# Layer two's last 256 rows in two chunks of 128, with one kept copy of the first MLP weight

## The chip, the cores and the metric

The kernel runs on one core of one Trainium2 chip. The metric is the device time of one execution in microseconds (us); the lower, the better.

## The reference

A transformer block is applied twice to x (2048 rows of 512 numbers), with the same weights both times:

```
x = x + A(layernorm(x))        A: 32 heads of width 16, softmax attention over all 2048 rows, then wo
x = x + B(layernorm(x))        B: relu(x @ w1) @ w2, inner width 1792
x = x + A(layernorm(x))
x = x + B(layernorm(x))
return x
```

Inputs and outputs are bfloat16. The attention needs 2 x 32 x 2048 x 2048 exponentials, which makes it the larger part of the work.

## The kernel before

**Tiles and chunks.** Rows are held in 16 tiles of 128 (`x_t`). A *chunk* is a run of row tiles that goes through attention, output projection, layer norm and MLP together. `chunks[l, j]` gives the first tile and the number of tiles. Layer one has four chunks of 512 rows. Layer two has two of 512 and then four of 256, (1,2) to (1,5); `LAST = 5` names the last one.

**Attention.** The attention of a chunk is cut into 8 *segments* (`t`) of four heads each, one head in each quarter of the array's rows; a segment runs over all 16 blocks of 128 keys. A *unit* is one head with 512 columns of scores: one key block for a chunk of 512 rows, two key blocks for a chunk of 256 (`both = QS // sg["w"]`). Three units fill a *slot*: TensorE computes the scores with 32-row weights (L1396), and ScalarE takes the exponential of up to 1536 columns in one instruction (L1405, `e`). In about half of the slots one of the three units goes to VectorE instead: it makes the exponential out of integer steps, two units at a time as a *pair* (`lin` L1090, `step` L1131, `cube` L1142 and L1146), and ScalarE's instruction is then 1024 wide. Such a unit is called a *half* below, as in the code. TensorE then multiplies by the values with 32-column weights (L983) and sums into the single PSUM bank `ps_o`; a pair needs three such products for one.

**End of a segment.** `finish_segment` copies `ps_o` to `u` (L897), sends the sums to a compact tile `c` by a DMA on SyncE's queue (L902), takes the reciprocal (L924), sends it back (L925) and spreads it over the partitions into `r`. The spreading is a DMA on GpSimd's queue (L927) or, for a segment that is `quick`, a shuffle on VectorE (L937). A multiplication (L913) then writes `ot`. There are three buffers `u`, `r` and `c`.

**The filler.** Output projection, layer norm and MLP of a chunk are cut into groups, which are put into the gaps that TensorE has while the attention of the next chunk runs (L446). `h_group` makes the first MLP product for one, or two, blocks of 128 inner columns; its weight `w1` comes from HBM, block by block, into four buffers (`load_w1`, L714), for every chunk again. `z_group` makes the second product with the resident `w2` (L768 adds it to x).

**The order.** All engines' instructions are put in order while the program is built, by a planner with a clock of its own for TensorE, VectorE and ScalarE. It holds constants for what a DMA takes: `C_LAG` for `c`, `U_LAG` for a quick `r`, `R_LAG` for an `r` that is spread by DMA. A VectorE step is put where its inputs are due by these constants. A planner's wrong guess leaves a wait in the order of an engine. It also decides for each pair whether VectorE can finish it before its segment ends. If TensorE is planned to be too idle, scores are computed more than once in a slot.

**The end.** The last chunk's projection, layer norm and MLP have no attention beside them. They are written out by hand (L1440 to L1528): the projection and the last segment's normalization (`direct`, L944 to L949), the statistics and the root, `half_part` (the second product of the second row tile of the chunk before, which TensorE does meanwhile), transposes, and then the MLP, one block of 128 inner columns after the other: `h` for block `ft`, relu on VectorE or ScalarE in turn, and the second product for block `ft - 1`. The `w1` blocks 4 to 13 for this are kept in the buffers of layer one's keys (`kt01`, `kt2`), which are free by then. They are loaded during the MLP of chunk (1,3), one block after each `h_group` (L747, `w1_to_load`).

Of the kernel before, what the change touches and what calls it, by code (L numbers as in the profile page):

```python
# [12 lines left out]
BF16 = mybir.dt.bfloat16  # L13
# [12 lines left out]
def kernel(  # L26
# [11 lines left out]
    P = 128  # L38
# [3 lines left out]
    S, D = x_flat.shape  # L42
# [4 lines left out]
    NF = DFF // P  # L47
    NTT = S // P
    NKB = S // P
    NDC = D // P  # L50
    QS = 512
# [25 lines left out]
    PE_TO_DVE, DVE_TO_PE, ACT_TO_PE, PE_TO_ACT = 220.0, 180.0, 240.0, 222.0  # L77
    DVE_TO_DVE, EVAC = 112.0, 612.0
    FLOOR = 0.56
    C_LAG, R_LAG, U_LAG = 3600.0, 10500.0, 3000.0  # L80
    VLAG = 1
    X_ISSUE, X_LAG = 1400.0, 7500.0
    RSTD_LAG = 4000.0
# [214 lines left out]
    def put_evac(cost, fn):  # L298
        evac.append((cost, now_pe[0] + PE_TO_DVE, fn))
# [159 lines left out]

    chunks = {(l, j): (j * TPC, TPC) for l in range(2) for j in range(NQS)}  # L460
    HALF = TPC // 2
    for n in range(4):
        chunks[1, 2 + n] = (2 * TPC + n * HALF, HALF)
    LAST = 5

    def columns(l, j):

# [118 lines left out]
    def ln_groups(tag, dst, at_column, n, war):  # L586
        groups = []
        for i in range(0, n, 2):
            hold = {}

            def piece(k):
                if not k % 2:
                    hold["b"] = bank()
                half = hold["b"].bitcast(BF16)[:, k % 2 * D : (k % 2 + 1) * D]
                ln_transpose(tag, k, half)
                if not k % 2:
                    return
                pt = hold["b"].bitcast(BF16).rearrange("p (i c f) -> p c i f", i=2, c=NDC)

                def fin():  # L600
                    a = at_column + (k - 1) * P
                    nc.vector.tensor_copy(
                        out=dst[:, :, a : a + 2 * P].rearrange("p c (i f) -> p c i f", i=2), in_=pt
                    )
                    for of in (k - 1, k):
                        mark(("xnT", tag, of))

                put_evac(609, fin)

            groups.append(  # L610
                group(
                    [(1.3, lambda k=k, piece=piece: piece(k)) for k in (i, i + 1)],
                    [("xT", tag, k) for k in (i, i + 1)] + [("xnT", tag, k) for k in (i, i + 1)],
                    [("xn", tag, k) for k in (i, i + 1)] + war,
                )
            )
        return groups

    def each(n, *key):
        return [key + (i,) for i in range(n)]  # L620
# [88 lines left out]

    def load_w1(n):  # L710

        if n < len(chunks) * NF - NF + NW1:
            ft = n % NF
            nc.sync.dma_start(  # L714
                out=w1buf[n % NW1][:],
                in_=B_w1[:, ft * P : (ft + 1) * P].rearrange("(c p) f -> p c f", p=P),
            )
            mark(("w1", n), "pe", 4000.0)

    w1_to_load = deque()  # L720

    def h_group(l, j, ft, war):
        n = (l * NQS + j) * NF + ft
        xj, a, w = columns(l, j)

        number = QS // w
        fts = range(ft, ft + number)
        made_here = [("h", l, j, f) for f in fts]

        def fin(b):  # L730
            out = htp[ft // 2][:, ft % 2 : ft % 2 + number, a : a + w]
            sums = b.rearrange("p (f q) -> p f q", f=number)
            if ending[0]:
                nc.scalar.activation(out=out, in_=sums, func=ACTF.Relu)
            else:
                nc.vector.tensor_scalar(  # L736
                    out=out, in0=sums, scalar1=0.0, scalar2=None, op0=ALU.max
                )
            for key in made_here:
                mark(key)  # L740

        def after():
            for f in range(number):
                load_w1(n + f + NW1)
            if w1_to_load:
                home, of = w1_to_load.popleft()
                nc.sync.dma_start(  # L747
                    out=home,
                    in_=B_w1[:, of * P : (of + 1) * P].rearrange("(c p) f -> p c f", p=P),
                )  # L750

        return mm_group(
            [
                (w1buf[(n + f) % NW1][:, c, :], xnT[xj][:, c, a : a + w])
                for f in range(number) for c in range(NDC)
            ],
            fin, made_here,
            each(w // P, "xnT", ("ln2", l, j)) + war + [("w1", n + f) for f in range(number)],
            after=after, wide_by=w, sums=number,
        )  # L760

    def z_group(l, j, i):
# [18 lines left out]
    def before(l, j):  # L781

        if (l, j) == (0, 0):
            return None
        if not j:
            return 0, NQS - 1
        rows = chunks[l, j][0] % TPC
        return max(
            (l, b) for b in range(j)
            if chunks[l, b][1] == TPC or chunks[l, b][0] % TPC == rows  # L790
        )

    w1_last = []
# [1 line left out]
    def rest_of_chunk(l, j):  # L795

        if (l, j) == (1, LAST - 2):
            for ft in range(NF):
                home = (
                    w1buf[((l * NQS + LAST) * NF + ft) % NW1] if ft < NW1  # L800
                    else (kt01 + kt2)[(ft - NW1) // 2][:, ft % 2, :].rearrange(
                        "p (c f) -> p c f", c=NDC
                    )
                )
                w1_last.append(home)
                if ft >= NW1:
                    w1_to_load.append((home, ft))
        b = before(l, j)
        xj, a, w = columns(l, j)
        n = w // P  # L810
        war_h = each(chunks[b][1], "z", *b) if b else []
        work[0:0] = [o_group(l, j, i) for i in range(n)] + ln_groups(
            ("ln2", l, j), xnT[xj], a, n, []
        )
        gs = [h_group(l, j, ft, war_h) for ft in range(0, NF, QS // w)]
        gs += [z_group(l, j, i) for i in range((l, j) == (1, LAST - 1), n)]
        if l == 0:
            if not by_dma(("ln1", 1, j)):
                gs += ln_groups(("ln1", 1, j), xnT[j], 0, TPC, [])
            gs.append(k_group(1, 0, j))  # L820
            gs += [v_group(1, kb) for kb in range(j * TPC, (j + 1) * TPC)]
            gs += [k_group(1, T, j) for T in range(1, 4)]
        return gs
# [43 lines left out]
    def finish_segment(sg, last):  # L867
# [50 lines left out]
                mark(("ot", l, j, t, i))  # L918

        ended[l, j] = ended.get((l, j), 0) + 1  # L920
        quick = ended[l, j] == NT or sg["load"] is not None and sg["busy"]

        def recip():
            nc.vector.reciprocal(out=c, in_=c)  # L924
# [35 lines left out]
        if last:  # L960
            last_steps.append(direct)
        elif sg is segs[-2]:
            task(3100, direct_all, ots + [("m", n)], war + [("u", n)])
        else:
            task(165, recip, [("r", n)], [("c", n)], place=0)
            ready = ("r", n)
            if quick:
                task(200 + 1.05 * width, spread, [("spread", n)], [ready])
                ready = ("spread", n)
            task(105 + 1.1 * width, lambda: mul(0, width), ots + [("m", n)], [ready] + war)  # L970
# [588 lines left out]
```

The softmax here doesn't subtract the row's maximum and nothing guards it: scores larger than these inputs give would overflow.

## Time and profile before

| what | value |
|---|---|
| time, median of 4 runs | 1586.87 us (1586.18 to 1589.21) |
| time of the profiled execution, and its span | 1586.18 us, 1584.3 us |
| ScalarE busy | 1545.3 us, 98% of the span |
| VectorE busy | 1506.3 us, 95% |
| TensorE busy | 1428.1 us, 90% |
| exponentials on ScalarE (L1405) | 1366: 663 of 1536 columns, 702 of 1024, one of 512 |
| from the end of the last exponential to the end of the span | 27.2 us |

The profile is a page on one execution. Its first part gives each engine's busy time, a later one the *chain of waits* that ended last, followed back from the last instruction. The *groups* list instructions by code line and shape with their busy time in us, the mean length of one in ns, and the idle time of the engine before them, with what ended it. The *timeline* lists instructions by start and length. Lengths of instructions that follow each other on one engine overlap[...]: what counts for a dense stretch is the distance from one start to the next.

### The profile page before, as it was taken

The numbers are of one execution on the slowest core, as the hardware profiler recorded it, in microseconds if no ns is written. First come the engines' busy times: TensorE is split into PE (matmuls) and PEld (weight loads), VectorE is DVE, ScalarE is ACT, GpSimd is POOL, SyncE is SP. The second block draws the span as 40 slices with busy tenths as digits, with TensorE's granted clock in tenths as the row PEclk, the third lists the DMA queues.
The fourth block names the chain that finished last, engine by engine and source line by source line (L and its number), as shares of the span: only waits on it lengthen the run. The fifth ranks groups of instructions, "written<-read, shape, count | busy, mean of one in ns | idle before, by whom it ended". The sixth has DMA issues, their size and how long they took to land.

```text
span 1584.3 us, 45170 instructions
## 1 busy us (share of the span) xinstructions
PE 1428.1 (90%) x19748; PEld 534.7 (34%) x19752; DVE 1506.3 (95%) x2910; ACT 1545.3 (98%) x1383; POOL 101.4 (6%) x240
## 2 busy tenths in 40 slices
PE   8888889998999989999899998888999999999897
PEld 3232223222233322322223222223234444545454
DVE  6899999999999999999899998899999999999995
ACT  6999999999999999999999999999999999999994
POOL 2000001001010010100100001001001000010100
PEclk9999999999999999999999999999999999999999
DMA  6001101111012120120101000000210111313020
GB/s 193 15 2 26 19 9 20 41 25 25 6 19 46 22 29 7 24 48 13 25 2 28 21 2 1 2 4 9 52 27 16 40 33 24 76 24 82 13 60 18
DMA packets 128885, 45.57 MB, mean 29 GB/s; under 512 B 117840, under 2 KB 125776, under 8 KB 128688
## 3 DMA queue, kind: packets, MB, share of 16 engines
q1 hardware_dynamic: 114752, 29.36, 8.6%
q0 software_dynamic: 12592, 12.02, 4.3%
q8 instruction: 154, 2.52, 0.7%
q10 hardware_dynamic: 1344, 1.31, 0.3%
q14 instruction: 43, 0.35, 0.1%
HBM read 24.38 MB, written 2.10 MB: 17 GB/s over the span
## 4 chain that ended last, share of the span: by engine, by line
ACT 80%; DVE 9%; PE 8%; issue 2%; DMA 2%; SPq 0%; ACTq 0%; DVEq 0%; POOLq 0%
ACT e L1405 80%; PE ps_s L1396 3%; DVE lin L1090 2%; PE ps_f L446 2%; PE ps_o L983 2%; DVE step L1131 1%; DVE cube L1146 1%; DVE cube L1142 1%; DMA r<-u 1%; PE ps_s L1458 1%; DVE ht L736 1%; DMA wqkv<-in_A_wqkv_dram 0%; DVE q L676 0%; DVE ot L913 0%; DVE stats L481 0%
## 5 line engine op out<-in xcount | busy, mean ns | idle before, releaser
L1405 ACT ACTIVATE e<-ps_s 128x1536 bf16<-128x1536 f32 (+1 forms) x1366 | 1536.7, 1361 | 7.1 <-PE ps_s L1396 6.5
L1396 PE MATMUL ps_s<-q,ktp 32*128 32x512 bf16 (+1 forms) x6136 | 606.6, 340 | 111.9 <-ACT e L1405 99.4
L983 PE MATMUL ps_o<-e,vaug 128*32 128x512 bf16 (+1 forms) x4236 | 500.3, 345 | 14.5 <-DVE u L897 8.3
L1090 DVE TENSOR_SCALAR lin<-ps_s 128x512 int16<-128x512 f32 x702 | 478.1, 685 | 26.0 <-PE ps_s L1396 19.6
L1396 PEld LDWEIGHTS <-ktp 32*128 32x128 bf16 x6136 | 199.5, 91 | 563.0 <-issue 418.8
L1131 DVE TENSOR_SCALAR step<-lin 128x1024 int16<-128x1024 int16 x702 | 275.1, 418 | 1.9 <-PE ps_o L983 0.9
L983 PEld LDWEIGHTS <-vaug 128*32 128x32 bf16 x6052 | 172.9, 94 | 301.7 <-issue 282.9
L1142 DVE TENSOR_TENSOR cube<-step 128x1024 f16<-128x1024 bf16 x351 | 238.2, 682 | 1.6 <-PE ps_o L983 0.2
L1146 DVE TENSOR_TENSOR cube<-cube,lin 128x1024 bf16<-128x1024 f16 x351 | 237.8, 679 | 0.0
L446 PE MATMUL ps_f<-w,ht 128*32 128x512 bf16 x1624 | 151.5, 381 | 1.8 <-DVE x L768 0.5
L446 PE MATMUL ps_f<-xnT,w 128*32 128x512 bf16 (+1 forms) x2016 | 146.3, 345 | 5.8 <-DVE ht L736 3.7
L983 PE MATMUL ps_o<-step,vaug 128*32 128x512 bf16 (+1 forms) x884 | 150.7, 340 | 0.0
L983 PE MATMUL ps_o<-cube,vthird 128*32 128x512 bf16 (+1 forms) x836 | 148.8, 339 | 0.0
L983 PE MATMUL ps_o<-lin,vaug 128*32 128x512 bf16 (+1 forms) x884 | 126.3, 340 | 4.6 <-DVE u L897 3.1
L927 POOL DMA_DIRECT2D r<-u x59 | 43.2, 732 | 1167.8 <-DVE lin L1090 338.1
L446 PE MATMUL ps_f<-xnT,wqkv 128*32 128x512 bf16 (+1 forms) x1312 | 108.3, 363 | 6.0 <-DVE ktp L626 1.1
L446 PE MATMUL ps_f<-wo,ot 128*32 128x512 bf16 x960 | 90.3, 380 | 1.2 <-DVE x L700 1.2
L736 DVE TENSOR_SCALAR ht<-ps_f 128x512 bf16<-128x512 f32 x105 | 71.9, 685 | 2.3 <-PE ps_f L446 1.5
L446 PEld LDWEIGHTS <-w 128*32 128x32 bf16 x2016 | 57.3, 96 | 34.0 <-issue 18.7
L676 DVE TENSOR_TENSOR q<-ps_f,masks 128x1024 bf16<-128x1024 f32 (+1 forms) x51 | 53.6, 1051 | 8.3 <-PE ps_f L446 7.3
L446 PEld LDWEIGHTS <-ht 128*32 128x32 bf16 x1624 | 46.7, 96 | 25.4 <-issue 11.9
L983 PEld LDWEIGHTS <-vthird 128*32 128x32 bf16 x836 | 43.5, 95 | 33.8 <-issue 29.0
(103 smaller groups left out, 607.8 us busy)
## 6 DMA issues: line engine op xcount, KB each, us to landing
w<-in_B_w_dram SPq DMA_DIRECT2D x130, 128.0 KB
r<-u POOLq DMA_DIRECT2D x32, 256.0 KB, 7.3
r<-u POOLq DMA_DIRECT2D x27, 128.0 KB, 4.9
out_dram<-x SPq DMA_DIRECT2D x16, 128.0 KB
x<-in_A_x_dram SPq DMA_DIRECT2D x14, 128.0 KB
w<-in_B_w_dram SPq DMA_DIRECT2D x1, 1792.0 KB
ktp<-in_B_w_dram SPq DMA_DIRECT2D x10, 128.0 KB
wqkv<-in_A_wqkv_dram ACTq DMA_DIRECT2D x2, 512.0 KB
```

The costliest lines, as they stand in the source:

```text
L446: nc.tensor.matmul(out[cols], lhsT[:, cols], rhs, start=i % k == 0, stop=i % k == k - 1, tile_position=(0, 32 * g), skip_group_check=True,)
L676: return nc.vector.tensor_mul(out=qbuf[n % 2][:, :, 0:w], in0=b.rearrange("p (e q) -> p e q", e=1).to_broadcast((P, 2, w)), in1=qmask.rear ...
L736: nc.vector.tensor_scalar(out=out, in0=sums, scalar1=0.0, scalar2=None, op0=ALU.max)
L927: nc.gpsimd.dma_start(out=r[:, 0:width], in_=bass.AP(tensor=sums.tensor, offset=sums.offset, ap=[list(sums.ap[0]), [0, 32], [1, width]],),)
L983: nc.tensor.matmul(ps_o[32 * g : 32 * g + 32, 0 : sg["w"]], values[:, 4 * sg["T"] + g, 2 * e : 2 * e + 32], rhs, start=g not in sg["begun" ...
L1090: first = nc.vector.tensor_scalar(out=lin[which][:, half * QS : (half + 1) * QS], in0=src, scalar1=EXP_BIAS, scalar2=0.0, op0=ALU.add, op1 ...
L1131: nc.vector.tensor_scalar(out=stair, in0=line, scalar1=keep, scalar2=put, op0=ALU.bitwise_and, op1=ALU.bitwise_or,)
L1142: (609, lambda: nc.vector.tensor_mul(out=power, in0=mantissa, in1=mantissa)),
L1146: (609, lambda: nc.vector.tensor_mul(out=power.bitcast(BF16), in0=power, in1=line.bitcast(BF16))),
L1396: nc.tensor.matmul(b[:, a : a + sg["w"]], kt[32 * g : 32 * g + 32, kc : kc + P], qbuf[sg["n"] % 2][32 * g : 32 * g + 32, sg["e"], 0 : sg[" ...
L1405: ex = nc.scalar.activation(out=eb[:, 0 : place[m]], in_=b[:, 0 : place[m]], func=ACTF.Exp, scale=1.0 / (LOG2E * UNIT),)
L1458: uses(nc.tensor.matmul(out, lhsT, rhs, start=first, stop=last), b, needs=needs)
```

## The change

Chunk (1,5), of 256 rows, becomes two chunks of 128, (1,5) and (1,6), and `LAST` is 6. A unit of such a chunk is one head with four key blocks of 128 columns. All segments of 128 rows are `quick`. `h_group` still makes two blocks of inner columns at once for them (`per_group`), so it fills half a bank. The MLPs of both chunks of 128 take `w1` blocks 4 to 13 from one kept copy, which is loaded during the MLP of chunk (1,4), two blocks after each `h_group`; the blocks 0 to 3 stay in the four `w1` buffers. `R_LAG` goes from 10500 to 13000, which bears on every segment of both layers whose `r` is spread by a DMA. The part of the diff in `ln_groups`, which lets a group hold one row tile, is cut here to its cost.

```diff
-    C_LAG, R_LAG, U_LAG = 3600.0, 10500.0, 3000.0
+    C_LAG, R_LAG, U_LAG = 3600.0, 13000.0, 3000.0
...
-    for n in range(4):
+    for n in range(3):
         chunks[1, 2 + n] = (2 * TPC + n * HALF, HALF)
-    LAST = 5
+    chunks[1, 5] = (3 * TPC + HALF, 1)
+    chunks[1, 6] = (3 * TPC + HALF + 1, 1)
+    LAST = 6
...
-                put_evac(609, fin)
+                put_evac(609 if m == 2 else 342, fin)
...
-        if n < len(chunks) * NF - NF + NW1:
+        if n < (NQS + LAST - 1) * NF + NW1:
...
+    def per_group(w):
+        return min(QS // w, 2)
+
...
-        number = QS // w
+        number = per_group(w)
...
-            if w1_to_load:
+            for _ in range(min(2, len(w1_to_load))):
                 home, of = w1_to_load.popleft()
+                mark(("kept", of), "pe", 6000.0)
                 nc.sync.dma_start(
                     out=home,
                     in_=B_w1[:, of * P : (of + 1) * P].rearrange("(c p) f -> p c f", p=P),
...
-                (w1buf[(n + f) % NW1][:, c, :], xnT[xj][:, c, a : a + w])
+                (
+                    (w1_last[ft + f] if (l, j) == (1, LAST - 1) else w1buf[(n + f) % NW1])[:, c, :],
+                    xnT[xj][:, c, a : a + w],
+                )
...
-            each(w // P, "xnT", ("ln2", l, j)) + war + [("w1", n + f) for f in range(number)],
-            after=after, wide_by=w, sums=number,
+            each(w // P, "xnT", ("ln2", l, j)) + war + [
+                ("kept", ft + f) if (l, j) == (1, LAST - 1) and ft + f >= NW1 else ("w1", n + f)
+                for f in range(number)
+            ],
+            after=after, wide_by=w, sums=number, cost=77 + 1.045 * number * w,
...
-                    w1buf[((l * NQS + LAST) * NF + ft) % NW1] if ft < NW1
+                    w1buf[((l * NQS + LAST - 1) * NF + ft) % NW1] if ft < NW1
...
-        gs = [h_group(l, j, ft, war_h) for ft in range(0, NF, QS // w)]
+        gs = [h_group(l, j, ft, war_h) for ft in range(0, NF, per_group(w))]
...
-        quick = ended[l, j] == NT or sg["load"] is not None and sg["busy"]
+        quick = ended[l, j] == NT or sg["load"] is not None and sg["busy"] or width == P
...
-            task(3100, direct_all, ots + [("m", n)], war + [("u", n)])
+            task(1560 * width // P, direct_all, ots + [("m", n)], war + [("u", n)])
```

In the order of the changed program, which shows no times, ScalarE has 669 exponentials of 1536 columns and 696 of 1024, and VectorE six halves fewer. In the last 86 slots, those of the last 256 rows, there are 35 of 1024 columns where there were 43. Two of the seven `h_group`s of chunk (1,5) are placed beside the attention of chunk (1,6); five stand after the last product with the values and have their relu on ScalarE.

## The prediction

> **What bounds the kernel now.** I read the busy shares, then the groups by shape (busy us, mean ns of one | idle us before), then the end of the chain of waits. ScalarE bounds everything but the two ends:
>
> ```profile
> PE 1428.1 (90%) x19748; PEld 534.7 (34%) x19752; DVE 1506.3 (95%) x2910; ACT 1545.3 (98%) x1383; POOL 101.4 (6%) x240
> L1405 ACT ACTIVATE e<-ps_s 128x1536 bf16<-128x1536 f32 x663 | 1004.6, 1577 | 4.6 <-PE ps_s L1396 4.1 <-PE ps_o L983 0.3
> L1405 ACT ACTIVATE e<-ps_s 128x1024 bf16<-128x1024 f32 x702 | 760.2, 1158 | 2.6 <-PE ps_s L1396 2.4
> ```
>
> Lengths overlap, so I take starts: in the trace the next exponential starts a median 1.330 us after one of 1536 columns, and 0.904 after one of 1024. These make 663 x 1.330 + 702 x 0.904 = 1516.4; from the first start (15.3) to the last end (1557.1) are 1541.8, so some 25 us are **lateness**, intervals longer than the median. A half given to VectorE saves ScalarE 0.426 us. What follows the last exponential is the second part of the time (start, length, what):
>
> ```profile
> 1549.64 7.47 ACT e L1405 x6
> ...
> 1558.04 3.63 PE ps_s L1458 x16
> ...
> 1561.70 0.59 ACT x L1468
> ...
> 1562.31 1.29 DVE stats L481 x2
> ...
> 1565.63 0.42 DVE xn L528
> ...
> 1566.10 0.73 PE ps_s L537 x8
> ...
> 1566.86 0.44 DVE xnT L1498
> ...
> 1567.43 0.61 PE ps_s L1458 x4
> ...
> 1580.33 0.69 DVE x L1525
> ```
>
> From 1567.43 to 1580.31 the MLP is matmul after matmul: TensorE bounds it, 0.87 us for each of 14 blocks.
>
> [...] eight transposes of 128 columns take 0.62, or (0.62 - 0.22)/7 = 0.057 apart, and six rounds of 4 matmuls with 32-column weights (256 columns) take 0.83, or (0.83 - 0.27)/5 = 0.11 a round. No row has 128 columns in the 32-wide layouts. [...] In the trace about 0.10 us pass between values and scores beyond the stream; the change doesn't alter how often this happens per slot. [...] one late `r` at 400.2 us holds up what stands behind it.
>
> ```profile
> 1232.48 0.62 PE L537 MATMUL ps_f<-ident,xn 128*128 128x128 bf16 x8
> 1522.90 0.83 PE L446 MATMUL ps_f<-xnT,w 128*32 128x256 bf16 x24
> 400.21 0.75 DVE L913 SCALAR_TENSOR_TENSOR ot<-u,masks,r 128x512 bf16<-128x512 f32 x1 [1.33 <-DMA r<-u]
> 402.06 5.38 ACT L1405 ACTIVATE e<-ps_s 128x1024 bf16<-128x1024 f32 x5 [0.69 <-PE ps_s L1396]
> ```
>
> **The change part by part.** *The end, T being the last exponential's end (1557.1 before).* The values end at about T+0.6 as before. Now five `h_group`s come first: each 8 rounds of 0.056, together 2.2, with their relu on an idle ScalarE. Then 8 projection matmuls of 0.216 (1.7) in place of 16 (3.5), with 0.1 for the layout. The last one starts at T+4.7, before at 1561.28 = T+4.2: **+0.5**. VectorE's shuffle (0.30, from 0.73 and 0.44 at 512 and 256 columns), reciprocal (0.95) and product (0.35) hide beside that. One statistics row less on the path: -0.6 (1.29 becomes 0.69). The root has 10 small steps for 11: -0.2. Transposes and copy: 4 for 8, but ScalarE's copy of 0.585 in place of VectorE's 0.42: -0.1. The MLP thus starts at T+9.9, before T+10.3. There a block costs TensorE 4 x 0.056 + 0.216 = 0.44, but now latency matters: from an h's last slot to its second product go 0.16 drain, 0.04, the relu (0.295, from 685 ns at 512 and 425 at 256 columns) and 0.06, so 0.56. In the order h(f+1), z(f), h(f+2), two blocks take 0.56 + 0.44, so 0.50 each. 14 blocks from first h to last z's end: 0.22 + 13 x 0.50 + 0.56 + 0.38 = 7.7, before 12.9: **-5.2**. The last copy is 0.585 for 0.69, the output DMA (3.3 to the span's end) stays. Sum: 0.5 - 0.6 - 0.2 - 0.1 - 5.2 - 0.1 = **-5.7**. Bounds: -7 (0.44 a block), -3.5 (0.60 a block and `h_group` rounds of 0.11).
>
> *Exponentials.* Six halves go back to ScalarE: 6 x 0.426 = **+2.6**, certain, since the order shows it. VectorE pays for segments: a segment of 128 rows costs it 0.28 (`u`) + 0.17 (`c`) + 0.30 (shuffle) + 0.32 (`ot`), 1.07, as much as one of 256 (0.416 + 0.193 + 0.462), and there are 16 for 8. That is +8.1 in a stage where VectorE is busy 98%; six halves are worth 6 x (0.685 + 0.418 + 0.68) = 10.7.
>
> *The stage of the last 256 rows.* Columns through TensorE stay the same. At 0.056 a round instead of 0.109/2 the rounds (1172 score matmuls, three to a round, and 1344 value matmuls, four: 727 rounds) cost 1.1 more, hidden in TensorE's slack. I put that at 10 us in this stage: 8% of it is neither stream nor layout change by my count of starts from 1285 to 1475, and some 2.4 are scores computed twice. Eight more evacuations of `ps_o` hold TensorE: it waited 11.3 us for L897 in 59 segments, 0.2 each, so 1.6, inside the slack. The exponentials were late by 1.4 per 95 us with 256 rows and 1.5 with 512, so halving rows cost nothing before. I take **+1.0**, bounds -1 and +8.
>
> *SyncE's queue and GpSimd's.* The eight `r` DMAs of a 256 chunk on GpSimd's queue go; there are 14 each of `c` and `u` DMAs for 6. The `w1` loads of chunk (1,4) come in fours after a group, before in threes; an issue took SyncE about 0.8 us in that phase of before (0.5 when it is free). `c` and `u` DMAs stand among them, landing 1.6 and 1.5 us after VectorE's step where the planner allows 3.6 and 3.0: room for two issues. In the 1.0.
>
> *`R_LAG`.* The stall shown at 400 us goes: around it exponentials were late by 1.8 (392 to 407). I take **-1.5**, bounds -1.8 and +2: the order changes from 112 us on, and other waits of the 25 us may come or go.
>
> Sum: -5.7 + 2.6 + 1.0 - 1.5 = **-3.6** against the profiled 1586.18, which gives 1582.6. That execution was 0.7 below the median of 1586.87, so I forecast 1583.3 for a median.
>
> **The rivals.** *A: the 32-wide layouts don't keep 56 ns at 128 columns.* For it: no row shows them, the instruction rate must rise[...]. Against: transposes keep 57, rounds of four at 256 columns start 3 or 4 ns apart. [...] It decides from 56 + 10/0.727 = 70 ns; it ends slower. *B: late `c` and `u` DMAs.* A shuffle now waits on VectorE for each, where before the waiting was GpSimd's. Some nine of them fall among the `w1` loads; each late by 1.7 (two issues more) and half of it reaching ScalarE: +7, 1590. *C: the reordering gives nothing*: `R_LAG`'s 1.5 is made up for by other waits, the stage costs 2: 1585.8, no change. *D: the end is as it is, but the MLP loop runs at 0.44 and the stall of 1.4 around 1500 us goes*: 1581.
>
> **How the numbers follow.** 0.2% is 3.2 us, about what a measurement of this kernel can tell from none. My forecast (1581 to 1586) has 0.60, D 0.06, C 0.16, A 0.09, B 0.09. Of the forecast's range three quarters lie below 1583.7, so faster is 0.45 + 0.06 = 0.51, same 0.15 + 0.16 = 0.31, slower 0.18. The range 1580 to 1590.5 takes in B and leaves out half of A and the far ends.
>
> **What would show it.** Right: 27.2 after the last exponential become 21.5; the last MLP runs at about 0.50 a block; no wait of VectorE for `r` near 400; score rounds of 128 columns 0.056 apart; and the last exponential ends within 3 us of 1557.1. Wrong: rounds above 0.07 and exponentials waiting for score matmuls from 1460 on (A), VectorE waits for `c` or `r` there (B), or lateness elsewhere that grows by more than 2 (C).

## The result and the profile after

| | before | after |
|---|---|---|
| time, median | 1588.41 us (56 runs) | 1585.85 us (35 runs) |
| ratio, with its 95% interval | | 0.9983 [0.9974, 0.9991] |
| profiled execution, and its span | 1586.18, 1584.3 us | 1584.80, 1582.9 us |
| last exponential's end, and from there to the span's end | 1557.11, 27.2 | 1560.03, 22.8 |
| lateness of the exponentials; of it in the last 86 slots | 24.6; 2.4 | 25.1; 4.6 |

The change gains 0.17%, or 2.7 us (1.4 to 4.1); 3.6 were forecast. (The four runs of the table further up had a median of 1586.87 for the kernel before; 1588.41 is that of 56.) Lateness is taken as in the prediction: what the intervals from one exponential's start to the next are longer than the median for their width.

The busy shares and the groups by shape of the changed kernel (busy us, mean ns of one | idle us before them) show the six halves that went back to ScalarE, 669 and 696 exponentials, and what the new 128-column steps cost:

```profile
PE 1432.5 (90%) x21308; PEld 552.0 (35%) x21311; DVE 1502.7 (95%) x2947; ACT 1549.2 (98%) x1387; POOL 95.6 (6%) x243
L1420 ACT ACTIVATE e<-ps_s 128x1536 bf16<-128x1536 f32 x669 | 1009.0, 1572 | 5.7 <-PE ps_s L1411 5.2 <-PE ps_o L998 0.3
L1420 ACT ACTIVATE e<-ps_s 128x1024 bf16<-128x1024 f32 x696 | 750.9, 1152 | 1.2 <-PE ps_s L1411 1.0
...
L912 DVE COPY u<-ps_o 128x128 f32<-128x128 f32 x15 | 4.3, 287 | 2.0 <-PE ps_o L998 1.9
...
L952 DVE STREAM_SHUFFLE r<-u 128x128 f32<-128x128 f32 x14 | 4.1, 296 | 0.0
...
L1527 DVE TENSOR_SCALAR ht<-ps_s 128x128 bf16<-128x128 f32 x7 | 2.0, 291 | 5.9 <-PE ps_s L1473 5.9
```

The chain of waits (start, length, what) at the end of the changed kernel:

```profile
1551.48 8.07 ACT e L1420 x6
...
1562.44 0.45 PE ps_f L446 x27
1562.89 1.68 issue
1564.57 0.23 PE ps_f L446
...
1565.17 1.69 PE ps_s L1473 x7
1566.88 0.59 ACT x L1483
1567.50 0.70 DVE stats L483
...
1570.66 0.41 PE ps_s L539 x4
1571.09 0.59 ACT xnT L1513
...
1571.73 0.40 PE ps_s L1473 x4
...
1578.99 0.40 PE ps_s L1473
...
1579.46 0.58 ACT x L1540
```

The MLP runs from 1571.73 to 1579.39, 7.66 us where it took 12.9. But the piece called "issue" is new: in the fifth `h_group` TensorE stands still for 1.68 us, and the profile shows nothing that it waits for.

Two rounds of 128 columns in the trace of after, the first of four rounds of three score matmuls, the second of four rounds of four value matmuls:

```profile
1490.44 0.40 PE L1411 MATMUL ps_s<-q,ktp 32*128 32x128 bf16 x12 [0.53 <-ACT e L1420]
1490.78 0.41 PE L998 MATMUL ps_o<-e,vaug 128*32 128x128 bf16 x16
```

The score rounds start at 1490.445, 0.500, 0.555 and 0.610, thus 0.055 apart; the value rounds are 0.056 to 0.066 apart. The layouts keep the rate, and rival A, for whose slower rate no trace gave a figure, has no place here. VectorE's waits for DMAs hold one line in after, the load of x at the start; before they also had a wait for `r` of 1.6 us. So no `c` or `r` DMA is late, and the second rival falls too.

```profile
DVE stats L483 <- DMA x<-in_A_x_dram: 1.3, 1, 1.3
```

TensorE's waits of after (us in total, times, longest) hold three lines for pauses without a releaser, in the filler and in the attention. The kernel before has one such line, of 0.2 us in all, in the last projection:

```profile
PE ps_f L446 <- issue: 1.7, 1, 1.7
...
PE ps_o L998 <- issue: 1.1, 2, 0.7
...
PE ps_s L1411 <- issue: 0.5, 2, 0.3
```

The two spans differ by -1.4: -4.4 at the end, +2.6 for the halves, +2.2 of lateness in the last 86 slots and -1.7 of lateness ahead of them, with 0.1 of rounding and of the first start.

### The profile page after: what moved, and what is told of

Same layout as the page of the kernel before. It is cut to its first block, busy times and chain, and to the rows that moved or that the text cites. A ratio compares the mean times of both kernels' runs of the same rounds, so it can differ in the third digit from the quotient of the medians.

```text
span 1582.9 us, 48353 instructions
## 1 busy us (share of the span) xinstructions
PE 1432.5 (90%) x21308; PEld 552.0 (35%) x21311; DVE 1502.7 (95%) x2947; ACT 1549.2 (98%) x1387; POOL 95.6 (6%) x243
## 4 chain that ended last, share of the span: by engine, by line
ACT 79%; PE 11%; DVE 8%; issue 2%; ACTq 0%; DVEq 0%
ACT e L1420 79%; PE ps_s L1411 4%; PE ps_f L446 3%; PE ps_o L998 3%; DVE lin L1105 2%; DVE step L1146 1%; DVE cube L1157 1%; DVE cube L1161 1%; PE ps_o L1179 1%; PE ps_s L1473 1%; DVE ht L744 0%; DVE q L681 0%; DVE ot L928 0%; DVE u L912 0%; DVE x L705 0%
## 5 line engine op out<-in xcount | busy, mean ns | idle before, releaser
L1420 ACT ACTIVATE e<-ps_s 128x1024 bf16<-128x1024 f32 (+1 forms) x1366 | 1539.9, 1358 | 6.9 <-PE ps_s L1411 6.3
L1411 PE MATMUL ps_s<-q,ktp 32*128 32x512 bf16 (+2 forms) x6699 | 609.0, 325 | 112.5 <-ACT e L1420 101.8
L998 PE MATMUL ps_o<-e,vaug 128*32 128x512 bf16 (+2 forms) x4682 | 496.0, 328 | 8.5 <-DVE u L912 2.7
L998 PE MATMUL ps_o<-step,vaug 128*32 128x512 bf16 (+2 forms) x950 | 159.0, 326 | 0.0
L446 PE MATMUL ps_f<-xnT,w 128*32 128x512 bf16 (+2 forms) x2080 | 148.1, 341 | 4.8 <-DVE ht L744 3.1
L998 PE MATMUL ps_o<-cube,vthird 128*32 128x512 bf16 (+2 forms) x888 | 143.2, 326 | 0.0
L998 PE MATMUL ps_o<-lin,vaug 128*32 128x512 bf16 (+2 forms) x950 | 124.4, 325 | 6.2 <-DVE u L912 3.7
L446 PE MATMUL ps_f<-xnT,wqkv 128*32 128x512 bf16 (+2 forms) x1376 | 108.4, 353 | 5.2 <-DVE ht L744 1.1
L744 DVE TENSOR_SCALAR ht<-ps_f 128x512 bf16<-128x512 f32 (+1 forms) x107 | 72.8, 681 | 2.9 <-PE ps_f L446 2.2
L681 DVE TENSOR_TENSOR q<-ps_f,masks 128x1024 bf16<-128x1024 f32 (+2 forms) x55 | 54.3, 986 | 7.8 <-PE ps_f L446 5.7
L998 PEld LDWEIGHTS <-vthird 128*32 128x32 bf16 x888 | 43.9, 95 | 28.5 <-issue 23.4
```

The costliest lines, as they stand in the source:

```text
L446: nc.tensor.matmul(out[cols], lhsT[:, cols], rhs, start=i % k == 0, stop=i % k == k - 1, tile_position=(0, 32 * g), skip_group_check=True,)
L681: return nc.vector.tensor_mul(out=qbuf[n % 2][:, :, 0:w], in0=b.rearrange("p (e q) -> p e q", e=1).to_broadcast((P, 2, w)), in1=qmask.rear ...
L744: nc.vector.tensor_scalar(out=out, in0=sums, scalar1=0.0, scalar2=None, op0=ALU.max)
L998: nc.tensor.matmul(ps_o[32 * g : 32 * g + 32, 0 : sg["w"]], values[:, 4 * sg["T"] + g, 2 * e : 2 * e + 32], rhs, start=g not in sg["begun" ...
L1411: nc.tensor.matmul(b[:, a : a + sg["w"]], kt[32 * g : 32 * g + 32, kc : kc + P], qbuf[sg["n"] % 2][32 * g : 32 * g + 32, sg["e"], 0 : sg[" ...
L1420: ex = nc.scalar.activation(out=eb[:, 0 : place[m]], in_=b[:, 0 : place[m]], func=ACTF.Exp, scale=1.0 / (LOG2E * UNIT),)
```

## The experiments

Two things were open: what the pauses of TensorE are, and which part of the change earns the 2.7 us. My theory of the pauses is that TensorE runs out of *instructions*. It is an inference from the traces. In that of after a packet of 16 KB on the instruction queue ran from 1562.28 to 1563.23, and TensorE resumed 1.34 later. The pages of after and before give that queue's packets, MB and share:

```profile
q8 instruction: 166, 2.72, 0.7%
q8 instruction: 154, 2.52, 0.7%
```

TensorE has 21308 matmuls and 21311 weight loads in after, 19748 and 19752 before: 256.7 and 256.5 of them to a packet. The five `h_group`s issue 160 matmuls and 160 weight loads; without the pause they would take some 2.3 us. The rival is a wait that the records don't show (an evacuation, or a late weight), which wouldn't follow the number of instructions.

All ratios are to the kernel before, run on the same chip (before: median 1589.36, 1588.82 and 1588.75 in the three groups of runs). The ratio is estimated from all runs and is not the quotient of the medians. *End* is the time from the last exponential's end to the span's end, in the one profiled execution. The expectations count otherwise: the end of after as 23.4, and lateness from 1475 us on (4.4 in after, 1.2 in e_rlag_alone).

Much of what differs from run to run goes with TensorE's mean granted clock, 0.976 to 1.000 in these runs. *At 0.995* is therefore an estimate of mine: a straight line through a kernel's runs, time against mean clock, read at 0.995. It holds to about 0.5 us (1.2 for e_rlag_once), and a change that itself moves the clock isn't judged by it. It gives 1588.5, 1588.7 and 1588.5 for the kernel before in the three groups, and 1586.8 for the changed kernel.

| kernel | median us | ratio [95%] | at 0.995 | end | lateness, last 86 slots |
|---|---|---|---|---|---|
| e_full | 1586.48 | 0.9973 [0.9961, 0.9986] | 1585.4 | 21.1 | 3.8 |
| e_double | 1590.88 | 1.0009 [0.9997, 1.0022] | 1590.9 | 28.9 | 4.2 |
| e_rlag_alone | 1585.78 | 0.9984 [0.9973, 0.9995] | 1585.3 | 28.2 | 1.4 |
| e_chunks_alone | 1592.46 | 1.0017 [1.0007, 1.0027] | 1590.9 | 21.0 | 4.3 |
| e_early | 1585.62 | 0.9977 [0.9969, 0.9985] | 1585.6 | 22.6 | 3.6 |
| e_split | 1587.93 | 0.9993 [0.9980, 1.0005] | 1586.2 | 26.9 | 3.1 |
| e_once | 1582.85 | 0.9963 [0.9950, 0.9976] | 1582.8 | 21.0 | 4.3 |
| e_best | 1582.88 | 0.9961 [0.9945, 0.9976] | 1583.2 | 20.0 | 3.1 |
| e_best_once | 1582.60 | 0.9974 [0.9961, 0.9987] | 1581.9 | 20.0 | 5.1 |
| e_rlag_once | 1587.97 | 0.9992 [0.9979, 1.0005] | 1585.2 | 28.8 | 1.4 |
| e_best_once_all | 1588.05 | 0.9997 [0.9988, 1.0007] | - | 21.6 | 1.5 |

### The pause at the end: fewer and more instructions

e_full is after, with the matmuls of the `h_group`s at the end in the full layout: one of 128 columns of weights in place of four of 32, so 80 instructions for 320.

```diff
                     out = b[:, i // k * wide_by : (i // k + 1) * wide_by]
+                    if ending[0]:
+                        nc.tensor.matmul(
+                            out, lhsT, rhs, start=i % k == 0, stop=i % k == k - 1,
+                            skip_group_check=True,
+                        )
+                        continue
                     for g in range(4):
```

> The changed kernel, with the five h_groups that stand after the last attention product written with 128-column weights: 80 instructions (weight loads and matmuls) instead of 320, the same columns. The order of all else is the same. Theory F (TensorE waits for its next block of instructions: the 1.68 us pause at 1562.9 us ends 1.3 us after a 16 KB packet of the instruction queue): the pause goes, and from the last exponential to the end of the span are 21.7 us instead of 23.4; the time is 1.7 us below the changed kernel, some 4 us below the kernel before. Rival (the pause is a wait for a kept weight, or belongs to the change of layout): it stays, 23.4.

The timeline of TensorE in e_full, from the first of these groups on:

```profile
1562.97 0.62 PE L445 MATMUL ps_s<-xnT,ktp 128*128 128x128 bf16 x8
1563.43 0.61 PE L445 MATMUL ps_f<-xnT,ktp 128*128 128x128 bf16 x8
1563.88 1.06 PE L445 MATMUL ps_s<-xnT,ktp 128*128 128x128 bf16 x16
1564.77 0.61 PE L445 MATMUL ps_f<-xnT,ktp 128*128 128x128 bf16 x8
1565.41 0.38 PE L1479 MATMUL ps_s<-x,ident 128*128 128x512 bf16 x1
```

The same work takes the same 0.45 for eight rounds, in 80 instructions, and the pause is gone; the end is 21.1. In the ratios the gain can't be told from noise (0.9973 beside 0.9983); at 0.995 it is 1.4 us.

e_double goes the other way: after, with each of these matmuls as two of 64 columns, 640 instructions for the same columns. Part of the sums is missing in this kernel's values; the number of its instructions is as said.

```diff
                     for g in range(4):
                         cols = slice(32 * g, 32 * g + 32)
-                        nc.tensor.matmul(
-                            out[cols], lhsT[:, cols], rhs, ...
+                        for h in range(1 + ending[0]):
+                            part = slice(64 * h, 64 * h + 64) if ending[0] else slice(None)
+                            nc.tensor.matmul(
+                                out[cols, part], lhsT[:, cols], rhs[:, part], ...
```

> The changed kernel, with each matmul of those five h_groups cut into two of 64 columns: 640 instructions instead of 320, and about the same time in the array[...]. Theory F: one or two more blocks of 256 instructions are used up in the burst, so there are one or two pauses more of 1 to 2 us each; the end takes 25 to 27 us instead of 23.4. Rival (a wait for data or for the layout): within 0.5 us of 23.4.

The timeline of TensorE in e_double:

```profile
1559.45 0.43 PE L448 MATMUL ps_s<-xnT,ktp 128*32 128x64 bf16 x29
1562.17 1.00 PE L448 MATMUL ps_s<-xnT,ktp 128*32 128x64 bf16 x95 [2.30 <-issue]
1562.99 0.20 PE L448 MATMUL ps_f<-xnT,ktp 128*32 128x64 bf16 x1
1562.99 0.19 PE L448 MATMUL ps_s<-xnT,ktp 128*32 128x64 bf16 x1
1563.00 0.20 PE L448 MATMUL ps_f<-xnT,ktp 128*32 128x64 bf16 x1
1563.01 0.19 PE L448 MATMUL ps_s<-xnT,ktp 128*32 128x64 bf16 x1
1563.02 0.43 PE L448 MATMUL ps_f<-xnT,ktp 128*32 128x64 bf16 x29
1565.92 0.66 PE L448 MATMUL ps_f<-xnT,ktp 128*32 128x64 bf16 x33 [2.47 <-issue]
```

Now there are two pauses, 2.30 and 2.47 us. Between them stand 95 + 1 + 1 + 1 + 1 + 29 = 128 matmuls; with one weight load each these are 256 instructions, for the 256.7 to a packet in after. 256 instructions took 3.75 us here from one resumption to the next, 1.28 of it work. The pauses follow the number of instructions, as the theory has it: none, one, and two, as the instructions go from 80 to 320 and 640. The kernel is slower than after, and the two intervals don't overlap.

The end grows by 6.1 to 28.9, more than the 25 to 27 expected, and the pauses are only 3.1 of that (4.77 for 1.68). The rest falls where TensorE ran at half its clock in this execution, from 1565.1 to 1572.0, in the windows of e_double (us, then PE, PEld, DVE, ACT and POOL busy, then the granted clock, DMA share and GB/s):

```profile
1565.20:1571.80 6.60, 5.66 (x45) 2.44 (x47) 0.61 (x1) 0.97 (x2) 0.00 (x0) 0.50 0.01 2
```

In the 3.4 us ahead of it TensorE had been busy for 0.37 of the time, with the second pause among them.

### Which part earns the gain

e_rlag_alone is before, with the new constant only. e_chunks_alone is after, with the old one.

```diff
-    C_LAG, R_LAG, U_LAG = 3600.0, 10500.0, 3000.0
+    C_LAG, R_LAG, U_LAG = 3600.0, 13000.0, 3000.0
```

> The kernel before with R_LAG at 13000 alone. The prediction gave this part -1.5 us (the stall at 400 us), with bounds of -1.8 and +2. In the order the number of halves is unchanged (702), so ScalarE's own work is that of before. Theory: exponentials are late by 23 us in all instead of 24.6 and the time is 1585 to 1588, -0.1%. Rival (the reordering makes as many waits as it takes away, as in the changed kernel, where they were late by 25.1): no difference.

> The changed kernel with R_LAG back at 10500: the two chunks of 128 alone. In the order there are 692 exponentials of 1024 columns (the changed kernel 696, before 702), so ScalarE has 4 x 0.426 = 1.7 us more than in the changed kernel, and three h_groups in the end instead of five (1.0 us less, and perhaps no pause there, 1.7 less). Theory: about equal to the changed kernel, -1 to +1 us. Rival (R_LAG carries the gain): as slow as the kernel before.

The constant alone is worth 0.16%, 2.5 us (0.8 to 4.3): as much as the whole change. It changes no number of halves (702 exponentials of 1024 columns, as before), only the order; and up to the last 86 slots the order of ScalarE and of VectorE is the same in after and in e_rlag_alone, so that these two tell what the chunks do. The wait for `r` near 400 is gone, and lateness in its profile is 20.5 (some 22 with the medians of before, which were 1 ns shorter) for 24.6; 1.6 of the difference stands in the 100 exponentials around 400 us. Some lateness on either side is the clock's and not the constant's. Before, TensorE had half its clock for 3.4 us at 963 and at 1499, and the exponentials there were late by 1.6 and 1.4. The windows of before:

```profile
963.00:966.00 3.00, 3.00 (x25) 0.60 (x24) 2.22 (x5) 2.23 (x2) 0.00 (x0) 0.50 0.00 0
1498.80:1502.20 3.40, 3.40 (x54) 2.08 (x56) 2.14 (x5) 2.72 (x2) 2.09 (x4) 0.50 0.03 6
```

e_rlag_alone has such pieces too, at 574 and 1007, where exponentials were late by 1.2 and 1.0, and at 1553, where one falls into the end (28.2 for 27.2):

```profile
1553.30:1556.50 3.20, 2.60 (x25) 1.38 (x24) 1.27 (x3) 0.82 (x2) 0.00 (x0) 0.50 0.03 5
```

The chunks without the constant are 0.17% slower, 2.7 us (1.1 to 4.3), which neither the theory nor the rival of the expectation had. For 1006 exponentials, some 1150 us, their order is that of before; then ten halves fewer fit (692 exponentials of 1024 columns, +4.3 us). Of 5.2 more lateness 1.9 is in the last 86 slots and 1.8 in the 274 ahead of them, above all 2.4 at 1169 to 1175, where this order puts 40 filler matmuls in a row ahead of scores that ScalarE waits for. The other 1.5 is at 400 us, at the wait that the constant takes away, shown in VectorE's waits of e_chunks_alone. The order there is that of before. That the wait is 2.3 here and 1.6 there, and that the clock was half from 403.6 to 407.0 here, is the execution's doing and not the edit's:

```profile
DVE ot L928 <- DMA r<-u: 2.3, 1, 2.3
```

The end is as short as in e_full (21.0; three `h_group`s are left for it, and a pause of 0.70 falls among them; five of 0.28 to 0.69 stand ahead of it, from 1515 us on). So the two chunks give 6 us at the end, and the planner's answer to them elsewhere costs more than that with the old `R_LAG`; with the new one they come out at nothing beside e_rlag_alone (0.9983 and 0.9984). At 0.995 the changed kernel stands 1.5 above e_rlag_alone, and e_full level with it: by this estimate the chunks cost 1.5 us as they are, and nothing without the pause at the end.

### What the last 256 rows lose

Against e_rlag_alone the last 86 slots of after are late by 3.2 more, against before by 2.2. Four pauses of TensorE fall among them, shown in its timeline of after:

```profile
1512.36 0.23 PE L998 MATMUL ps_o<-cube,vaug 128*32 128x128 bf16 x1 [0.71 <-issue]
...
1516.11 0.23 PE L1411 MATMUL ps_s<-q,ktp 32*128 32x128 bf16 x1 [0.15 <-issue]
...
1520.40 0.30 PE L1411 MATMUL ps_s<-q,ktp 32*128 32x128 bf16 x6 [0.32 <-issue]
...
1524.42 0.23 PE L998 MATMUL ps_o<-e,vaug 128*32 128x128 bf16 x1 [0.36 <-issue]
```

They come four us apart, each 1.35 to 1.6 after the end of a packet on the instruction queue, and the exponentials at those places are late by 0.88, 0.14, 0.21 and 0.46, together 1.7. Such packets come every 4.1 us in this stage, every 6.5 before: not far from the 3.75 that 256 instructions took in e_double. Two kernels were to tell whether the number of instructions does this, or what else crowds the stage. e_split is e_rlag_alone with the score and value matmuls of its last chunk cut in two, 2616 instructions more and nothing else changed. (The first product with the values of each head stays whole.)

```diff
+                cut = P if (sg["l"], sg["j"]) == (1, LAST) else sg["w"]
+                for at_c in range(0, sg["w"], cut):
-                nc.tensor.matmul(b[:, a : a + sg["w"]], ...)
+                    nc.tensor.matmul(b[:, a + at_c : a + at_c + cut], ...)
```

> The kernel before with R_LAG at 13000 (as e_rlag_alone), and in its last chunk of 256 rows each score matmul, and each value matmul but the first of a sum, cut into two of 128 columns: 2616 more instructions of TensorE, where the changed kernel has 3048 more; segments, VectorE's and ScalarE's work and the order stay those of e_rlag_alone. Theory F (in the last 256 rows TensorE runs out of instructions): pauses without a wait appear from 1460 us on, lateness after 1475 us goes from 1.2 us to 3 to 4.5, the time is 2 to 3 us above e_rlag_alone. Rival (the lateness of the changed kernel there comes from twice as many segments on VectorE): no pauses, lateness 1.2 to 1.7, the time of e_rlag_alone.

Packets come every 4.1 us there too, but TensorE has no such pause. The lateness is 3.1, of it 1.5 at one wait for a `w1` load, shown in its timeline:

```profile
1522.71 0.62 PE L446 MATMUL ps_f<-xnT,w 128*32 128x256 bf16 x16 [1.33 <-DMA w<-in_B_w_dram]
```

e_early is after, with the kept copy of `w1` loaded one chunk earlier, beside the MLP of chunk (1,3), one block after each group in place of two. Before the change its like was loaded there too.

```diff
-        if (l, j) == (1, LAST - 2):
+        if (l, j) == (1, LAST - 3):
...
-            for _ in range(min(2, len(w1_to_load))):
+            for _ in range(min(1 if j == LAST - 3 else 2, len(w1_to_load))):
```

> The changed kernel with the kept weight loaded one MLP earlier (from chunk (1,3)'s list on), so that beside chunk (1,5)'s attention SyncE issues pairs of loads and no fours. The order on TensorE, VectorE and ScalarE is the same. Theory L (the loads in fours slow down the fetching of instructions, and so make the pauses of TensorE at 1512, 1516, 1520 and 1524 us): those pauses shrink to half or less, lateness after 1475 us goes from 4.4 us to about 3, and the time is 1.4 us below the changed kernel. Rival (the number of instructions alone makes them): pauses and lateness as in the changed kernel, no difference.

Pauses of 0.27, 0.16 and 0.30 are left in the stage, it is late by 3.6, and the pause at the end is still there (1.41). The time, 0.9977, can't be told from 0.9983. The pauses also vary where nothing was changed: e_full has the order and the loads of after in this stage, and shows two, of 0.61 and 0.16. So theory L is not shown, and neither kernel settles the stage by its time.

A count of the instructions does. In the trace of after, 257, 255 and 256 matmuls and weight loads start between one of the four pauses and the next, and 2558 between the fourth and the pause at the end, two short of ten times 256. TensorE's waits of after, e_full, e_early, e_double, e_chunks_alone, e_best and e_best_once list 27 pauses without a releaser. Counted from the start of each program, 26 of them stand at the same remainder by 256, within five; the other is 0.22 us in e_double's last projection, at half clock. So the pauses of the stage are of one kind with that of the end: they stand at one place in the count of 256, and TensorE went on 1.2 to 1.6 us after the end of a packet. At the other places of this count in the stage of after it shows no such pause; the packet had ended 1.35 to 5.6 us before. By the same count packets were 3.5 us or more ahead in the kernel before, and 1.55 or more in e_split, near to the 1.2 to 1.6 of the pauses.

The pauses are 1.7 of the 3.2. Of the rest, 0.9 is repeated scores, where a slot's 12 score matmuls are done twice, as in the timeline of after:

```profile
1481.64 1.05 PE L1411 MATMUL ps_s<-q,ktp 32*128 32x128 bf16 x24 [0.61 <-ACT e L1420]
...
1482.73 1.45 ACT L1420 ACTIVATE e<-ps_s 128x1536 bf16<-128x1536 f32 x1 [0.22 <-PE ps_s L1411]
```

The bank came free late (a wait of 0.61), and the exponential then waits for both copies. At this slot and at one like it near 1500 the exponentials are late by 0.46 and 0.45 in after, and by 0.44 to 0.46 in e_full, e_early, e_double and e_best, which keep the repeats; in the three kernels below that leave them out they are late by 0.01 at most. Another 0.40, at 1487, follows a wait of 0.58 of TensorE for the evacuation `u`.

### Leaving out repeated scores, and versions that combine

In a slot where the planner finds TensorE too idle, scores are computed twice. e_once leaves the repeats out where rows are 128: fewer instructions for the same result.

```diff
-        for _ in range(times):
+        for again in range(times):
             pe_run("s", 1, s_ready)
+            if again and now[0][0]["w"] == P:
+                continue
```

> The changed kernel without the repeated scores in the slots of 128 rows (the planner still counts them, so the order is the same): 148 score matmuls less, 296 instructions of some 6200. Theory F: a pause or two less, lateness after 1475 us down by 0.3 to 1 us. Rival (the repeats keep the granted clock up, and that is worth more): clock below 0.98 somewhere after 1460 us, and the time the same or up to 3 us longer.

It reaches 0.9963, and at 0.995 it is 4.0 us below the changed kernel. No pause is left in its trace, at the end (21.0) or in the stage: with 296 instructions fewer every 256th falls elsewhere. The stage shows 4.3 of lateness, but 3.0 of it at exponentials in a piece at half clock, from 1489.4 to 1503.0; the 1.3 left are about what e_rlag_alone has. The windows of e_once:

```profile
1490.00:1502.00 12.00, 11.59 (x282) 8.45 (x282) 10.12 (x28) 10.01 (x10) 0.00 (x0) 0.50 0.03 3
```

The rival of the expectation may have a part in this: in the 3.4 us ahead of that piece TensorE was busy for 0.64 of the time, where in after, with the repeats, it was 0.80 at the same exponentials; e_best_once has the same piece there.

e_best puts e_full and e_early together, and lets the second product of the last MLP follow two blocks behind the first in place of one.

```diff
-    for ft in range(NF + 1):
+    for ft in range(NF + 2):
...
-        if ft:
+        if ft > 1:
...
-                    banks[i], ht[ft - 1][:, part(i)], w2[:, ft - 1, :],
-                    False, ft == NF, "h",
+                    banks[i], ht[ft - 2][:, part(i)], w2[:, ft - 2, :],
+                    False, ft == NF + 1, "h",
```

> e_full and e_early together, and in the MLP at the end the second product two blocks behind the first instead of one, so that TensorE need not wait for the relu. From the separate parts: -1.7 (no pause in the end), -0.8 (14 blocks at 0.44 instead of 0.50 us), and 0 to -1.4 for the loads: 2.5 to 4 us below the changed kernel, about 0.996 of the kernel before; 20.4 us from the last exponential to the end of the span. Rival (blocks stay at 0.50 because TensorE is held up by the banks): 21.1.

Its chain of waits at the end:

```profile
1555.60 1.06 PE ps_o L1004 x50
...
1561.16 0.59 ACT x L1489
...
1565.99 0.83 PE ps_s L1479 x12
...
1570.96 1.65 PE ps_s L1479 x13
...
1572.68 0.59 ACT x L1546
```

The MLP takes 6.6 from 1565.99, 0.44 a block in place of 0.50, so the difference was latency, as the prediction had it; the end is 20.0. At 0.9961 this is the lowest ratio of all, though its interval overlaps that of the change as it is.

Three more carried the repeats further: e_best_once is e_best with e_once's edit; e_rlag_once is e_rlag_alone without repeats in its last chunk; e_best_once_all is e_best without repeats in all of layer two.

```diff
+            if again and now[0][0]["w"] == P:                     # e_best_once
+            if again and (first["l"], first["j"]) == (1, LAST):   # e_rlag_once
+            if again and first["l"]:                              # e_best_once_all
+                continue
```

> e_best and e_once together: full-width weights in the five h_groups of the end, kept loads one MLP earlier, the second product two blocks behind, no repeated scores in the slots of 128 rows. If the gains are of different waits (the end; the pauses beside the attention) they add: 4 to 6 us below the changed kernel, about 0.9945 of the kernel before. If e_once gained mostly because the burst in the end met no block boundary, most of it is in e_best already: 0.996. The end takes 20.0 us, as in e_best.

> The kernel before with R_LAG at 13000 and no repeated scores in its last chunk of 256 rows. Theory F (repeats cost only where TensorE is short of instructions, with 128 columns): the time of e_rlag_alone, 0.998 of the kernel before. Rival (repeats cost in any chunk, because they keep TensorE from the fillers): lateness after 1475 us stays near 1.2 us, but the last exponential ends 1 us or more earlier, 0.997 or less.

> e_best_once with no repeated scores in all slots of layer two. Theory F: no further gain, since chunks of 512 and 256 rows show no pauses; 0 to +5 us against e_best_once if the granted clock falls where TensorE has less to do (the clock in the middle of layer two below 0.99). Rival: each repeat left out gives something, 1 us or more below e_best_once.

None gains by its ratio: 0.9974 for 0.9961, 0.9992 for 0.9984, and 0.9997, above 0.9961 by more than the intervals. But the clock has a large part in these three. The runs of e_best_once are twelve of 1578.6 to 1582.6 us at a mean clock of 0.994 to 0.998 and ten of 1586.5 to 1589.9 at 0.985 to 0.991; its median is the lowest of all, and at 0.995 it is 1.2 below e_best. So leaving out the repeats with 128 rows probably helps here too. e_rlag_once is level with e_rlag_alone at 0.995, as its theory had it: with 256 columns the repeats in the last chunk held nothing up. e_best_once_all had a mean clock of 0.976 to 0.990, e_best 0.988 to 1.000, and in its profile four pieces at half clock, 20.5 us in all, stand between 1034 and 1102. Its expectation allowed for such a loss where TensorE has less to do: from 1090 to 1190 us it has 1151 matmuls, before 1234. That the one makes the other is not shown. How much the repeats of the wider chunks are worth by it was not measured.

## Why the prediction was right, point by point

| term | forecast | profiles of before and after |
|---|---|---|
| end | -5.7 | -4.4 |
| six halves | +2.6 | +2.6 |
| stage of the last 256 rows | +1.0 | +2.2 |
| `R_LAG` and the rest of the lateness | -1.5 | -1.7 |
| sum | -3.6 | -1.4 (with rounding); time -2.7 (-1.4 to -4.1) |

*The end: right in its steps but one.* The MLP took 7.66 for a forecast of 7.7, and e_best's 0.44 shows that the term for latency was real. In after 0.55 pass from an h's last slot to its second product (1573.02 to 1573.57), for a forecast of 0.56; what the prediction calls drain, 0.16, is the length of a matmul's record beyond its slot (0.272 and 0.109 in the MLP of before). The `h_group`s took their 2.2 and the 128-column steps their estimated lengths (`u` 287 ns, shuffle 296, relu 291 and 277). The step that failed is the first: the five `h_group`s had their 2.2 of work and a pause besides. The MLP starts 11.7 after the last exponential for a forecast of 9.9, 1.68 of it the pause that e_full takes away and of which e_double has two, 0.1 a slightly slower root (10 steps of 0.195). The output DMA gives 0.5 back (2.8 for 3.3). I had counted what each instruction takes, and not how many there are.

*The halves: right,* to the instruction. In VectorE's account beside it a sum is off: sixteen segments for eight at 1.07 cost 8.6 more, not 8.1, which the six halves (10.7) still cover.

*The stage: mis-sized.* +1.0 became +2.2 beside before, +3.2 beside e_rlag_alone; both lie within the bounds. Of the 3.2, 1.7 is the four pauses, for which the prediction had no term, and 0.9 the repeated scores, which it had counted as slack of TensorE: at two slots ScalarE waited for them. Of the causes that it priced, rounds kept 0.056 and no DMA was waited for. The evacuations held TensorE for 2.1 us in this stage (six waits; 1.2 and three before), and after one of these waits an exponential was late by 0.40.

*`R_LAG`: right in its mechanism, larger in its share.* The wait near 400 is gone, and lateness around it is 1.5 less in after and 1.6 less in e_rlag_alone; the remaining lateness ahead of the last slots, pieces at half clock among it, about cancels. Alone the constant measures 2.5 (0.8 to 4.3). It carries the whole net gain: the rest of the change, forecast at -5.7 + 2.6 + 1.0 = -2.1, measures about nothing beside e_rlag_alone. Not foreseen was that the two chunks lose time without it.

*The sum: near in part by luck.* 2.7 (1.4 to 4.1) takes in the forecast of 3.6, but two errors offset each other: the constant gave 2.5 for 1.5, and all the rest about nothing for -2.1. The profiles differ by 1.4 and not 3.6, and the estimates at 0.995 by some 1.8. The prediction's signs came out mixed: rounds, the MLP's 0.50 and the wait near 400 as it said, the last exponential's end 2.9 late where 3 was allowed, and the end 22.8 where 21.5 was said.

*The rivals.* A and B fell with the rounds and VectorE's waits. C, whose sum is -1.1, is nearer to the profiles' -1.4 than the forecast is; it had the stage's 2, and its sign, lateness that grows by more than 2, came there. But the gain of `R_LAG` was not eaten up by other waits, as C had it. D's MLP at 0.44 needed another order (e_best), and its stall around 1500 was a piece at half clock in before; after has none there.

## What to carry to other kernels

When an edit makes pieces smaller, count the instructions per microsecond, not only the time of each: here TensorE stood still for 1.68 us in a burst of 160 short matmuls with 160 weight loads, and for 2.30 and 2.47 in one of 640 instructions, with no wait in the records. In e_full one matmul with 128 columns of weights did the work of four with 32, in the same 0.45 us for eight rounds, with a quarter of the instructions and no pause. Work that fills idle time wasn't free either: the repeated scores added instructions, and at two slots the engine that bounds the kernel waited for them. When several edits go in together, run each alone: here a constant of the planner earned what the large edit was credited with, and the large edit lost time without it.

## What was not expected of the hardware

- TensorE paused with no wait in the records: 1.68 us in a burst of 320 instructions, 2.30 and 2.47 in one of 640 with 256 between the two, none with 80. Shorter pauses, 0.15 to 0.71, stood 256 instructions apart in a stage that took some 4.1 us for each 256. From one resumption to the next 256 instructions took 3.75 us in e_double, and 3.75, 4.29 and 4.02 in after. TensorE resumed 1.2 to 1.6 us after the end of a 16 KB packet on the instruction queue. That it had used up its instructions is my inference from these counts. In e_once, with 296 instructions fewer, there was no pause.
- The granted clock fell to half for 3.4 us, or for two, three or four times that, up to seven times in a profiled execution (3.4 us at 963 in before, 13.6 from 1489 in e_once). In 41 of 42 such pieces, over all thirteen profiles, TensorE had been busy for only 0.37 to 0.72 of the 3.4 us just ahead (0.88 in the other), though not every such stretch was followed by one. Many places return: 383 to 385 us in five kernels, 573 to 576 in six. Around eleven pieces of 3.4 us beside exponentials lateness was 0.8 to 1.6.
- Executions of after with a mean clock of 0.998 and more took 1582 to 1585 us, one with 0.988 took 1594: the spread of the runs is mostly this, and single profiles can't settle differences of 2 us.
